# A chunk-attention, top-1 MoE and swish-MLP kernel: the gate in five batches, its matmuls one step later, and the second MLP's first scales and sums beside the last expert tiles

## The chip, the core and the metric

The kernel runs on one core of one Trainium2 chip. The core has a TensorE for matrix products (PE in the rows; PEld is its weight load), a VectorE (DVE), a ScalarE (ACT), a GpSimd (POOL) and a SyncE (SP). Each takes its own instructions in order, and they wait for one another by semaphores. DMA queues move data; here SP and POOL issue them. The metric is the device time of one execution in microseconds; lower is better.

## The reference, cut to what matters

```python
# q, k, v: (8, 8, 576, 64), chunks of 64 positions
scores = 0.125 * q_chunk @ k_chunk.T                 # softmax over 64 keys
x = softmax(scores) @ v_chunk                        # -> tokens: (4608, 512)

xn = x / (norm(x) + 1e-6); en = emb / (norm(emb) + 1e-6)
logits = xn @ en.T / tau                             # (4608, 8)
e = argmax(logits); gate = max of softmax(logits)    # top-1
y = gate * (relu(x @ w1[e]) @ w2[e])                 # 512 -> 1024 -> 512

h = y @ w_in                                         # 512 -> 2048
out = (h / (1 + exp(-1.702 * h))) @ w_out            # 2048 -> 512
```

## The kernel before, in words

Everything is one program without outer loops over data on the chip: its instructions are written out, and each engine executes its own list in the order in which the code emits them.

**The attention front.** A loop over n handles 36 blocks of 128 tokens, as a software pipeline: step n transposes q or k (`emit_T`, matmul L307), makes the scores of block n (L334), transposes the probabilities of n-1 (L357), multiplies those of n-2 with v (L379), and finishes the token tile of n-3 (`end_X`: `x` is scaled into `xr` on POOL at L417 and L418). `emit_XT` (L431) transposes that tile for the gate, `evac_XT` (L439) copies it to `xTa`, and `end_L` issues its gate logits, eight small products with the normalised expert embeddings (L454), into the bank `gb`. Before, `end_L` stands at the end of the same step.

**The gate.** The tiles are gated in batches (`batches`: first tile, count). For a batch, `norm` (16 small DVE operations) and `gate` (some 18 small DVE operations, rank matmuls at L545, an exponential) are generators; `drip` emits about ten pieces of them a step between the operations of attention. The gate's last result is the place of each token in a list sorted by expert. `place` (L494) writes it for one tile by an indirect DMA of POOL into one of two tables `mtab`, even tiles to one, odd tiles to the other, and a write waits until the previous one to its table has landed. `scat` emits one such write. After the loop come the last batch's pieces, with the parts of the first expert tiles' `mm1` and `mm2` in between, and then the last writes (`while scats: scat()`), before `find(3)`.

**The expert stage.** 39 tiles of 128 sorted tokens. `find(i)` (POOL, L851) reads the tables, `fetch(i)` (POOL, L864) gathers the tokens, `turn(i)` (SP) transposes them, `mm1(i)` (PE, L888, 96 products) is relu'd into `hT` by ACT (L895) and DVE (L896), `mm2` (PE, L921, 24 products) is scaled by ACT (L947) and DVE (L948) and scattered back by POOL (L955). `mm2(i-1)` stands behind `mm1(i)`. `swap` splits the next expert's weights into high and low halves where the expert changes (ACT L786, DVE L791; the weights are staged in `stg` and `stgB`).

**The decode.** Beside it, `big_split`, a generator of 32 blocks, turns the second MLP's float64 weights into float16 halves, one block an iteration from i=3 on (`next(dec)`, at the end of the iteration). Block b issues a magnitude for block b+1 on ACT (L1124), `after(b-1)` and four DVE operations. `after` casts on ACT (L1118) and subtracts on POOL (L1127), and the casts wait for the subtractions:

```python
if i == 0:   put(B11, f[0])                          # i is b % 4; put is a cast, then a subtraction
elif i == 1: minus(f[0], f[1], f[0]); put(T1, f[0])
elif i == 2: put(B22, f[2]); minus(f[1], f[2], f[1]); put(T3, f[1])
             minus(f[0], f[2], f[0]); put(T2, f[0])
else:        put(B21, f[3]); minus(f[0], f[3], f[0]); put(T4, f[0])
```

From block 16 on, `after` is one `put`. At iteration LASTD = 36 (NSURE is 3, SURE is 39) the decode ends, its memory is given back, and `prep(0)` loads the first group of the second MLP.

**The second MLP.** Nine groups of 512 tokens. `scales(j)` puts the tokens' scales on a diagonal (DVE L1284), spreads them over the partitions by one matmul (L1286) and copies that (ACT). `sums(j)` makes sums of quarters of the group's tokens (DVE L1297, L1312 to L1324) and splits each into halves `S` (ACT L1301, POOL L1302). `up(j, s)` multiplies them by the weights (PE L1338) and `down` goes back (PE L1451 to L1453). For group 0 both stand before the loop, behind the last expert tile and a `tc.If` (L1236) that catches lists of more than 39 tiles; for the others they stand beside `down` of the group before.

## Time and profile before

| what | value |
|---|---|
| time, median of 3 runs | 1449.27 us (1449.14 to 1451.39) |
| profiled execution, its time | 1442.4 us |
| its span (first to last instruction) | 1440.7 us |
| PE busy in the span | 1300.4 us (90%) |
| DVE, ACT, POOL busy | 855.3, 640.1, 722.7 us |
| mean granted TensorE clock | 0.958 of full speed |

The profile is one execution of the kernel. Its span leaves out 1.7 us of its own time. An engine that is busy 90% of the span bounds it on the whole; what a part of the program waits for is read from its own stretch of the timeline. In timelines, a number in brackets is the time that the engine stood idle before an instruction, and the arrow names what released it.

### The profile page before, as it was taken

How to read it: one execution, taken by the hardware profiler on the slowest of the kernel's cores; microseconds unless marked ns; L12 is line 12 of the kernel's file. 1: busy time of each engine (PE TensorE's matmuls, PEld its weight loads, DVE VectorE, ACT ScalarE, POOL GpSimd, SP SyncE). 2: the span in 40 equal slices, each digit the busy share in tenths (PEclk: the TensorE clock that was granted, in tenths of full speed). 3: DMA queues.
4: the chain of work that ended last, by engine and by line, in shares of the span. 5: the costliest groups of instructions: out<-in, count | busy, mean ns of one | idle time of the engine just before them, and what ended most of it. 6: DMA issues, size and time to landing. Idle time of an engine off the chain costs nothing.

```text
span 1440.7 us, 31953 instructions
## 1 busy us (share of the span) xinstructions
PE 1300.4 (90%) x12802; PEld 915.1 (64%) x12802; DVE 855.3 (59%) x1681; ACT 640.1 (44%) x1125; POOL 722.7 (50%) x648
## 2 busy tenths in 40 slices
...
GB/s 209 216 191 173 167 131 143 68 211 132 209 209 128 162 167 183 255 215 146 69 38 16 45 1 59 2 37 23 23 38 15 45 16 45 9 51 1 30 1 30
DMA packets 196279, 140.71 MB, mean 98 GB/s; under 512 B 129928, under 2 KB 167816, under 8 KB 196112
## 3 DMA queue, kind: packets, MB, share of 16 engines
...
## 4 chain that ended last, share of the span: by engine, by line
PE 50%; DMA 3%; issue 0%; DVE 0%; POOL 0%; ACT 0%; POOLq 0%; DVEq 0%; ACTq 0%
PE pb L1338 6%; PE pd L1338 6%; PE pa L1338 6%; DMA xg<-xs,mt 3%; PE pc L1338 3%; PE gb L1338 3%; PE pa L1453 2%; PE pa L1452 2%; PE pa L1451 2%; PE pd L1451 2%; PE pd L1452 2%; PE pd L1453 2%; PE pb L1452 2%; PE pb L1451 2%; PE pb L1453 2%; PE gb L1452 1%
## 5 line engine op out<-in xcount | busy, mean ns | idle before, releaser
L1338 PEld LDWEIGHTS <-wS 128*128 128x128 f16 x3024 | 297.1, 98 | 42.4 <-issue 5.2
L888 PE MATMUL ph<-xTm,w1HL 128*128 128x128 f16 x3744 | 234.7, 226 | 38.8 <-DMA xTm<-xg 8.1
L888 PEld LDWEIGHTS <-w1HL 128*128 128x128 f16 x3744 | 225.5, 101 | 55.8 <-issue 19.5
L1363 POOL TENSOR_TENSOR w2HL<-z,w1HL 128x512 f16<-128x512 f32 x144 | 217.2, 1524 | 82.8 <-ACT w1HL L1362 81.3
L921 PE MATMUL py<-w2HL,hT 128*128 128x512 f16 x936 | 208.2, 379 | 0.0
L921 PEld LDWEIGHTS <-hT 128*128 128x128 f16 x936 | 89.9, 98 | 101.5
L1458 POOL DMA_INDIRECT out_dram<-y,idc x36 | 35.4, 982 | 235.0 <-ACT y L1457 195.2
L1356 ACT ACTIVATE z<-z 128x512 f32<-128x512 f32 x144 | 88.3, 629 | 107.0 <-DVE z L1353 54.4
L955 POOL DMA_INDIRECT ys<-y,idx_y x39 | 39.1, 1002 | 146.7 <-ACT hT L895 60.1
L1359 DVE TENSOR_TENSOR z<-stgB,z 128x512 f32<-128x512 f32 x108 | 105.3, 1001 | 0.0
L851 POOL DMA_INDIRECT mt<-mtab,idx_g x78 | 88.3, 1132 | 32.9 <-issue 19.7
L1453 PEld LDWEIGHTS <-w2HL 128*128 128x128 f16 x576 | 56.4, 98 | 67.9
L1451 PEld LDWEIGHTS <-w1HL 128*128 128x128 f16 x576 | 56.4, 98 | 67.0
L1452 PEld LDWEIGHTS <-w1HL 128*128 128x128 f16 x576 | 56.4, 98 | 67.0
L1362 ACT ACTIVATE w1HL<-z 128x512 f16<-128x512 f32 x144 | 86.9, 625 | 8.4 <-DVE z L1359 8.4
L417 POOL TENSOR_TENSOR x<-x,sx_all 128x512 f32<-128x512 f32 x33 | 34.3, 1039 | 85.9 <-DVE rd L387 36.8
L896 DVE SCALAR_TENSOR_TENSOR hT<-ph,hT 128x512 f16<-128x512 f32 x78 | 51.0, 683 | 42.8 <-ACT hT L895 40.5
L1175 DVE SCALAR_TENSOR_TENSOR d_f<-raw_o,d_t 128x512 int32<-128x512 int32 x32 | 68.2, 2132 | 3.1
L895 ACT ACTIVATE hT<-ph 128x512 f16<-128x512 f32 x78 | 44.3, 590 | 53.9 <-PE ph L888 49.8
L1384 DVE TENSOR_TENSOR stgB<-stgB,pb 128x512 f32<-128x512 f32 x28 | 19.1, 684 | 81.3 <-PE pb L1338 76.1
L934 ACT ACTIVATE ysq<-py 128x512 f16<-128x512 f32 x39 | 23.1, 593 | 93.8 <-PE py L921 76.2
L1384 DVE TENSOR_TENSOR stgB<-stgB,pd 128x512 f32<-128x512 f32 x27 | 18.5, 684 | 76.4 <-PE pd L1338 76.4
...
## 6 DMA issues: line engine op xcount, KB each, us to landing
...
```

The source lines that it names most:

```text
L851: nc.gpsimd.indirect_dma_start(out=mt_t[i][a][:, :], out_offset=None, in_=mtab[a][:, :], in_offset=bass.IndirectOffsetOnAxis(ap=idx_g[:, i ...
L888: nc.tensor.matmul(p[:, f % 4], wt[:, c, fs], xT[:, a, :], start=(c == 0 and a == 0 and wt is w1H), stop=(c == KD - 1 and wt is w1L),)
L921: nc.tensor.matmul(p, hT[:, a, :], wt[:, c, :], start=st, stop=sp)
L1175: nc.vector.scalar_tensor_tensor(out=fi, in0=hi, scalar=-(1 << 31), in1=t, op0=ALU.bitwise_and, op1=ALU.bitwise_or)
L1338: nc.tensor.matmul(dst, wS[a][:, o, kc, fs], rhs(b, kc), start=first and ab == 0 and kc == 0 and n == 0, stop=(kc == 1 and n == 2), skip_g ...
L1356: nc.scalar.activation(out=z, in_=z, func=AF.Sigmoid, scale=1.702 * 2.0 ** -G_EXP)
L1359: nc.vector.tensor_tensor(out=z, in0=c, in1=z, op=ALU.mult)
L1362: nc.scalar.activation(out=dst[0], in_=z, func=AF.Copy)
L1363: nc.gpsimd.tensor_tensor(out=dst[1], in0=z, in1=dst[0], op=ALU.subtract)
L1451: nc.tensor.matmul(p, gT[0][:, h, c, tt], wo[0][:, c, :], start=(c == 0), stop=False)
L1452: nc.tensor.matmul(p, gT[0][:, h, c, tt], wo[1][:, c, :], start=False, stop=False)
L1453: nc.tensor.matmul(p, gT[1][:, h, c, tt], wo[0][:, c, :], start=False, stop=(c == KG - 1))
```

## The change

Five things are edited in the first two stages and at the seam to the third.

- The gate's batches become five, of 10, 10, 4, 6 and 6 tiles, where they were seven, of 8, 8 and five of 4. The small tiles and the regions of the bank `gb` grow to match. `norm` has one operation fewer: `itau` is multiplied in by `gate`.
- `end_L` of a tile moves from the end of its step to the start of the next one, behind `emit_T` (for n up to 34).
- `scat` is called up to twice at its second place of a step, and the queue of waiting writes is emptied from n = 28 on, where it was 30.
- LASTD becomes 33: `next(dec)` is called twice at i = 6, 8 and 10, so the decode ends, and `prep(0)` starts, three tiles earlier.
- `scales` is cut into `diagonal` and `spread`, and `sums` yields its results to `parts`. For group 0, `diagonal(0)` stands at the end of i = 36, `spread(0)` before `mm2` of tile 36, `early_sums()` at the end of i = 37, and `parts(0)` before `mm2` of tile 37; nothing of them is left behind the `tc.If`. The sums of group 0 lie in memory of their own.

```diff
@@ -439,7 +439,7 @@
...
-    batches = [(0, 8), (8, 8), (16, 4), (20, 4), (24, 4), (28, 4), (32, 4)]
+    batches = [(0, 10), (10, 10), (20, 4), (24, 6), (30, 6)]
@@ -447,7 +447,7 @@
         bi = [j for j, (a, n) in enumerate(batches) if a <= t < a + n][0]
...
-            o = 0 if bi + 1 < len(batches) else 208
+            o = 0 if bi + 1 < len(batches) else 416
             lg_t[bi] = gb[:, o:o + 2 * n * NE].rearrange("p (a e) -> p a e", a=n)
@@ -471,17 +471,15 @@
         yield from rsqrt(y, small("t", n, I32), small("a", n), ssc)
         nc.vector.tensor_tensor(out=y, in0=y, in1=ssc, op=ALU.mult)
         yield
-        nc.vector.tensor_scalar(y, y, 1e-6, None, op0=ALU.add)
+        nc.vector.scalar_tensor_tensor(
+            out=y, in0=y, scalar=1e-6, in1=sx_all[:, t0:t0 + n], op0=ALU.add, op1=ALU.mult
+        )
         yield
...
         isx = is_all[:, t0:t0 + n]
         nc.vector.tensor_scalar(
             isx.bitcast(I32), si_all[:, t0:t0 + n], float((BIAS - X_TOP) << 23), None, op0=ALU.add
-        )
-        yield
-        nc.vector.scalar_tensor_tensor(
-            out=y, in0=y, scalar=itau[:, 0:1], in1=isx, op0=ALU.mult, op1=ALU.mult
         )
         yield
@@ -511,8 +509,9 @@
         l = small("l", n, w=NE)
         nc.vector.tensor_tensor(out=l, in0=lg[:, 0:n, 0:NE], in1=dl, op=ALU.add)
         yield
-        nc.vector.tensor_tensor(
-            out=l, in0=l, in1=rn_all[:, T].unsqueeze(2).to_broadcast([128, n, NE]), op=ALU.mult
+        nc.vector.scalar_tensor_tensor(
+            out=l, in0=l, scalar=itau[:, 0:1], in1=rn_all[:, T].unsqueeze(2).to_broadcast([128, n, NE]),
+            op0=ALU.mult, op1=ALU.mult,
         )
         yield
@@ -539,7 +538,7 @@
         ex = small("ex", n, w=NE)
...
         yield "pe"
-        rkf = gb[:, 128:128 + n * NE]
+        rkf = gb[:, 272:272 + n * NE]
         rk = rkf.rearrange("p (a e) -> p a e", a=n)
         ohf = oh.rearrange("p a e -> p (a e)")
         nc.tensor.matmul(rkf, tri16, ohf, start=True, stop=False)
@@ -990,6 +989,7 @@
     front[LATE + 3] = LATE - 1
     back = {LATE + 2: LATE - 2}
     back.update((t + 3, t) for t in range(LATE, NTILE))
+    turned = []
     for n in range(NTILE + 3):
         now[0] = n
         u, step = n // QR + 1, n % QR
@@ -1003,6 +1003,9 @@
         on(n - 3, emit_sq)
         for f in ev[1]:
             f()
+        if n <= NTILE - 2:
+            for t in turned:
+                end_L(t)
         turned = []
         if n - 1 in back:
             evac_XT(back[n - 1])
@@ -1021,16 +1024,18 @@
         on(n - 1, emit_PT, evac_PT)
         on(n - 2, emit_PV)
         issue_v(v_due(n))
-        if len(scats) > (4 if n < 30 else 0):
-            scat()
+        for _ in range(2):
+            if len(scats) > (4 if n < 28 else 0):
+                scat()
         on(n, exp_S)
         drip(1)
         on(n - 2, emit_x)
         drip(1)
         if n in back:
             emit_XT(back[n])
-        for t in sorted(turned):
-            end_L(t)
+        if n >= NTILE - 2:
+            for t in sorted(turned):
+                end_L(t)
@@ -1192,8 +1197,70 @@
     for b in range(NRAW):
         big_load(b)
     dec = big_split()
+    S_t = [t.bitcast(F16).rearrange("p (l s k t) -> p l s k t", l=2, s=4, k=2) for t in stg_i]
+    def diagonal(j):
+        idc = id_t[j]
+        iv = idc.bitcast(F32)
+        so = mlp.tile([128, 4], F32, tag="so", name="so", bufs=2)
+        nc.vector.tensor_scalar(so, iv[:, :, 1], 2.0 ** (-2 * G_EXP), None, op0=ALU.mult)
+        dg = mlp.tile([128, 4, 128], BF16, tag="dg", name="dg")
+        for a in range(4):
+            nc.vector.tensor_scalar(dg[:, a], identB, iv[:, a, 1:2], None, op0=ALU.mult)
+        id_t[j] = (idc, so)
+        R_t[j] = dg
+    def spread(j, p):
+        nc.tensor.matmul(p, onesB, R_t[j].rearrange("p a t -> p (a t)"), start=True, stop=True)
+        R = mlp.tile([128, 2, 256], BF16, tag="R", name="R", bufs=2)
+        nc.scalar.activation(out=R.rearrange("p a t -> p (a t)"), in_=p, func=AF.Copy)
+        R_t[j] = R
+    def parts(j, i, x):
+        S = S_t[j % 2]
+        nc.scalar.activation(out=S[:, 0, i], in_=x, func=AF.Copy)
+        nc.gpsimd.tensor_tensor(out=S[:, 1, i], in0=x, in1=S[:, 0, i], op=ALU.subtract)
+    def sums(j, quarters, new):
+        yT = yT_t[j]
+        def quarter(r):
+            t = quarters(r).rearrange("p (k t) -> p k t", k=2)
+            nc.vector.tensor_tensor(out=t, in0=yT[:, 2 * r:2 * r + 2], in1=yT[:, KD + 2 * r:KD + 2 * r + 2], op=ALU.add)
+            return t[:, :, 0:256], t[:, :, 256:512]
+        def put(i, x, y, op):
+            o = new(i).rearrange("p (k t) -> p k t", k=2)
+            nc.vector.tensor_tensor(out=o, in0=x, in1=y, op=op)
+            return o
+        a11, a21 = quarter(0)
+        yield
+        a12, a22 = quarter(1)
+        yield
+        s1 = put(0, a21, a22, ALU.add)
+        yield 0, s1
+        s2 = put(1, s1, a11, ALU.subtract)
+        yield 1, s2
+        yield 2, put(2, a11, a21, ALU.subtract)
+        yield 3, put(3, a12, s2, ALU.subtract)
+    def early_sums():
+        w = mlp.tile([128, 2 * KD, 512], F16, tag="yT", name="yT", bufs=2)
+        wf = w.rearrange("p a t -> p (a t)").bitcast(F32).rearrange("p (q t) -> p q t", q=2)
+        z = [
+            mlp.tile([128, 2, 256], F32, tag="z", name="z", bufs=4).rearrange("p a t -> p (a t)")
+            for _ in range(4)
+        ]
+        return [x for x in sums(0, lambda r: wf[:, r], lambda i: z[i]) if x]
     yT_t, id_t, R_t = {}, {}, {}
-    LASTD = NSURE + 33
+    LASTD = NSURE + 30
     for i in range(NSURE, SURE):
         mm1(i)
         if i + 2 < SURE:
@@ -1204,11 +1271,17 @@
             find(i + 4)
         if i + 1 < SURE:
             swap(i + 1, 1)
+        if i == SURE - 1:
+            for n, x in s_0:
+                parts(0, n, x)
+        if i == SURE - 2:
+            spread(0, gb)
         mm2_part(i - 1, 0, KF)
         swap(i, 2)
         mm2_evac(i - 1)
         if i < LASTD:
-            next(dec, None)
+            for _ in range(2 if i in (6, 8, 10) else 1):
+                next(dec, None)
         if i == LASTD:
             next(dec, None)
             dec_stack.close()
@@ -1231,6 +1304,10 @@
                 yT_t[j], id_t[j] = yT, idc
             prep(0)
+        if i == SURE - 3:
+            diagonal(0)
+        if i == SURE - 2:
+            s_0 = early_sums()
     mm2(SURE - 1)
     last = reg(more_i[0:1, 0:1], [ENG.SP, ENG.Activation, ENG.DVE, ENG.PE, ENG.Pool], 1)
@@ -1272,58 +1348,6 @@
...
-    def scales(j):
...
-        p = bank()
-        nc.tensor.matmul(p, onesB, dg.rearrange("p a t -> p (a t)"), start=True, stop=True)
-        R = mlp.tile([128, 2, 256], BF16, tag="R", name="R", bufs=2)
-        nc.scalar.activation(out=R.rearrange("p a t -> p (a t)"), in_=p, func=AF.Copy)
-        R_t[j], id_t[j] = R, (idc, so)
...
-    def sums(j):
-        yT, S = yT_t[j], S_t[j % 2]
...
@@ -1460,22 +1484,28 @@
             in_=o[:, :], in_offset=None,
         )
-    scales(0)
-    for _ in sums(0):
-        pass
+    def spare_q(r):
+        return mem("hT", F32, 1024)
+    def spare_s(i):
+        return mem(("xg", "xTm")[i // 2], F32, 512)
     for j in range(NG):
         for s in range(4):
             up(j, s)
             if s == 0 and j + 1 < NG:
                 prep(j + 1)
         flush()
-        more = sums(j + 1) if j + 1 < NG else iter(())
+        more = sums(j + 1, spare_q, spare_s) if j + 1 < NG else iter(())
         for n, (t, part) in enumerate((t, part) for th in range(2) for part in range(4) for t in (2 * th, 2 * th + 1)):
             down(j, t, part)
             if n > 1:
-                next(more, None)
+                x = next(more, None)
+                if x:
+                    parts(j + 1, *x)
             if n == 10 and j + 1 < NG:
-                scales(j + 1)
+                diagonal(j + 1)
+                spread(j + 1, bank())
```

Three places show how the instructions stand. First PE's list at a step of the front: `db` is the product with v, `tp` a transposition of k, `gb` the gate's logits from the token tile `xTa`, `xr` the next token tile. Before:

```order
L357 MATMUL ptp<-identF,P 128x128 x4
L379 MATMUL db<-vt_91,PT 64x65 x16
L454 LDWEIGHTS xTa
L454 MATMUL gb<-enT,xTa 128x16
...
L454 LDWEIGHTS xTa
L454 MATMUL gb<-enT,xTa 128x16
L307 MATMUL tp<-identF,ku 128x128 x8
L431 LDWEIGHTS xr
L431 MATMUL sp_169<-ident_88,xr 128x128
```

and now:

```order
L357 MATMUL ptp<-identF,P 128x128 x4
L379 MATMUL db<-vt_91,PT 64x65 x16
L307 MATMUL tp<-identF,ku 128x128 x8
L454 LDWEIGHTS xTa
L454 MATMUL gb<-enT,xTa 128x16
...
L454 LDWEIGHTS xTa
L454 MATMUL gb<-enT,xTa 128x16
L431 LDWEIGHTS xr
L431 MATMUL sp_169<-ident_88,xr 128x128
```

The eight pairs of the gate's logits have moved behind the transpositions of the next step.

Second POOL's list at the end of the gate: `mtab` is a table that a placement writes, L851 (now L850) is `find(3)`, and L864 (now L863) the gather of `fetch(3)`. Before:

```order
L789 TENSOR_TENSOR w2HL<-stg_82,w2HL 128x512
L494 DMA mtab_76<-meta,pi_all 36864x2
L494 DMA mtab_77<-meta,pi_all 36864x2
L494 DMA mtab_76<-meta,pi_all 36864x2
L494 DMA mtab_77<-meta,pi_all 36864x2
L851 DMA mt_4372<-mtab_76,idx_g 128x2
L851 DMA mt_4373<-mtab_77,idx_g 128x2
L955 DMA ys<-y,idx_y 4736x1032
L858 TENSOR_TENSOR mt_4372<-mt_4372,mt_4373 128x2
L864 DMA xg<-xs,mt_4372 128x1024
```

and now:

```order
L788 TENSOR_TENSOR w2HL<-stg_82,w2HL 128x512
L492 DMA mtab_76<-meta,pi_all 36864x2
L492 DMA mtab_77<-meta,pi_all 36864x2
L492 DMA mtab_76<-meta,pi_all 36864x2
L492 DMA mtab_77<-meta,pi_all 36864x2
L492 DMA mtab_76<-meta,pi_all 36864x2
L492 DMA mtab_77<-meta,pi_all 36864x2
L850 DMA mt_4271<-mtab_76,idx_g 128x2
L850 DMA mt_4272<-mtab_77,idx_g 128x2
L954 DMA ys<-y,idx_y 4736x1032
L857 TENSOR_TENSOR mt_4271<-mt_4271,mt_4272 128x2
L863 DMA xg<-xs,mt_4271 128x1024
```

Between the last weight operation and `find(3)` stand six placements where there were four; the rows behind them are the same.

Third ACT's list at the end of iteration 8 of the expert loop: `y` is the result of tile 7, `d_t` a magnitude and `wS` a cast of the decode, and `hT` the relu of tile 9, which `mm2(9)` reads and whose evacuation frees the bank for `mm1(10)`. Before:

```order
L830 UNCONDITIONAL_BRANCH
L934 ACTIVATE ysq,ysc<-py_5956 128x512
L947 ACTIVATE y<-py_5956,ysc 128x512
L1124 ACTIVATE d_t<-raw_o_4584 128x512
L1118 ACTIVATE wS_4575<-d_f 128x512
L895 ACTIVATE hT<-ph 128x512 x2
L762 TENSOR_LOAD fl_i
```

and now:

```order
L829 UNCONDITIONAL_BRANCH
L933 ACTIVATE ysq,ysc<-py_5865 128x512
L946 ACTIVATE y<-py_5865,ysc 128x512
L1129 ACTIVATE d_t<-raw_o_4484 128x512
L1123 ACTIVATE wS_4474<-d_f 128x512
L1129 ACTIVATE d_t<-raw_o_4485 128x512
L1123 ACTIVATE wS_4474<-d_f 128x512 x3
L894 ACTIVATE hT<-ph 128x512 x2
L761 TENSOR_LOAD fl_i
```

Between the result of tile 7 and the relu of tile 9 stand two magnitudes and four casts, where one of each stood.

## Rows read from the trace of the kernel before

**Rows 1.** Head of the profile page: span, engines.

```profile
span 1440.7 us, 31953 instructions
...
PE 1300.4 (90%) x12802; PEld 915.1 (64%) x12802; DVE 855.3 (59%) x1681; ACT 640.1 (44%) x1125; POOL 722.7 (50%) x648
```

**Rows 2.** Windows by stage: us, busy (count) of each engine, TensorE clock, DMA.

```profile
39.00:215.00 176.00, 125.34 (x2793) 106.52 (x2793) 147.29 (x445) 129.17 (x246) 92.69 (x88) 0.87 0.81 175
215.00:254.00 39.00, 20.06 (x296) 17.50 (x296) 26.57 (x79) 14.90 (x26) 30.04 (x30) 0.69 0.56 142
...
284.00:529.00 245.00, 214.52 (x2275) 155.95 (x2273) 151.74 (x280) 94.45 (x164) 145.20 (x146) 0.94 0.65 180
...
734.00:1440.00 706.00, 700.48 (x4721) 461.64 (x4718) 349.54 (x448) 271.70 (x471) 337.09 (x248) 1.00 0.10 25
```

**Rows 3.** Windows of two steps of the front.

```profile
57.00:61.50 4.50, 3.57 (x93) 3.09 (x94) 3.65 (x9) 4.23 (x9) 2.21 (x3) 1.00 0.81 205
...
66.90:72.40 5.50, 3.73 (x81) 3.30 (x72) 5.43 (x20) 4.37 (x9) 2.19 (x2) 0.83 0.61 156
```

**Rows 4.** Waits of PE, 39 to 215 us: total, times, longest.

```profile
PE gb L454 <- DVE xTa L439: 11.7, 10, 1.8
PE gb L454 <- DVE si_all L405: 10.9, 11, 1.9
```

**Rows 5.** Timeline of PE, one step: start, duration, [idle before <-releaser].

```profile
54.62 0.36 PE L454 MATMUL gb<-enT,xTa 128*128 128x16 f16 x8 [0.93 <-DVE si_all L405]
54.83 1.07 PE L307 MATMUL tp<-identF,qu 128*128 128x128 f32 x8
```

**Rows 6.** Timeline of POOL, end of the gate.

```profile
262.80 1.34 POOL L494 DMA_INDIRECT mtab<-meta,pi_all  x1 [0.82 <-DVE ttmp L647]
...
266.89 1.31 POOL L494 DMA_INDIRECT mtab<-meta,pi_all  x1 [1.49 <-DMA mtab<-meta,pi_all]
...
272.30 0.99 POOL L851 DMA_INDIRECT mt<-mtab,idx_g  x1 [2.83 <-DVE hT L896]
...
276.98 1.01 POOL L864 DMA_INDIRECT xg<-xs,mt  x1 [0.63 <-issue]
```

**Rows 7.** Timeline of PE, expert tiles 3, 6, 8 and 10.

```profile
283.67 8.02 PE L888 MATMUL ph<-xTm,w1HL 128*128 128x128 f16 x96 [6.60 <-DVE y L951]
...
328.94 5.52 PE L888 MATMUL ph<-xTm,w1HL 128*128 128x128 f16 x96
...
352.72 0.28 PE L888 MATMUL ph<-xTm,w1HL 128*128 128x128 f16 x2 [2.54 <-ACT w1HL L786]
...
378.42 0.27 PE L888 MATMUL ph<-xTm,w1HL 128*128 128x128 f16 x2 [1.12 <-DVE hT L896]
```

**Rows 8.** Timeline of ACT, iterations 6 and 8 of the expert loop.

```profile
342.37 0.61 ACT L1118 ACTIVATE wS<-d_f 128x512 f16<-128x512 f32 x1
...
350.66 1.06 ACT L895 ACTIVATE hT<-ph 128x512 f16<-128x512 f32 x2
...
374.32 1.07 ACT L895 ACTIVATE hT<-ph 128x512 f16<-128x512 f32 x2
```

**Rows 9.** Timeline of PE, expert tiles 19 to 22.

```profile
487.60 0.61 PE L888 MATMUL ph<-xTm,w1HL 128*128 128x128 f16 x8
...
502.43 0.27 PE L888 MATMUL ph<-xTm,w1HL 128*128 128x128 f16 x2 [3.78 <-DVE hT L896]
...
530.01 5.19 PE L888 MATMUL ph<-xTm,w1HL 128*128 128x128 f16 x90
```

**Rows 10.** Timeline of PE, transition to the second MLP.

```profile
721.58 0.39 PE L1286 MATMUL pa<-ysq,onesB 128*128 128x512 bf16 x1 [4.33 <-DVE ysq L1284]
722.19 2.50 PE L1338 MATMUL pc<-yT,wS 128*128 128x256 f16 x12 [0.22 <-issue]
...
733.44 1.47 PE L1338 MATMUL pb<-yT,wS 128*128 128x256 f16 x12
```

**Rows 11.** Timeline of DVE, the same stretch.

```profile
726.20 0.69 DVE L1312 TENSOR_TENSOR xg<-hT 128x512 f32<-128x512 f32 x1 [2.41 <-DMA mt<-mtab,idx_g]
```

41 lines of the change are left out of this document (2 added, 39 removed).

## The prediction, as it was put on record before the changed kernel was run

> **What bounds the kernel now.** I read the head of the page first: PE is busy 1300.4 of 1440.7 us [rows 1], so on the whole the products bound the kernel, and only what lies in the other 140 us, or makes PE slower, can be won or lost. The windows by stage say where these lie [rows 2]. In the second MLP, from 734 us on, PE is busy 700.48 of 706 us: nothing of this change can shorten that. In the front (39 to 215 us) PE is busy 125.34 of 176 us, and DVE, with 147.29 us, is the engine most in use; in the gate's end (215 to 254) it is POOL, with 30.04 of 39. In the first half of the expert stage (284 to 529) PE stands still for 30 of 245 us. So each edit is priced in its own stretch.
>
> **The front.** Here 30 steps take 176 us, 5.87 us each. A step without pieces of the gate takes 4.50 us with 9 operations on DVE (3.65 us busy) and ACT busy for 4.23; a step full of them takes 5.50 with 20 operations, DVE busy 5.43 [rows 3]. Eleven small operations thus cost 1.0 us, 0.09 each. All 445 DVE operations are 30 x 9 = 270 of attention and 175 of the gate: 30 x 4.50 + 175 x 0.09 = 151 us. The remaining 25 us are stalls. PE's table of waits names most of them: the gate's products stand at the end of a step and wait for the token tile just copied, 11.7 us in 10 waits and 10.9 in 11 [rows 4], and behind them in PE's list stand the next step's transpositions, as in the row of 0.93 us of idle time [rows 5].
>
> What the change does to it: fewer batches. By 215 us, five and a half norms and five gates had run; now four norms and three gates, one operation shorter each: I count 126 operations of the gate for 175, that is 49 x 0.09 = 4.4 us less on DVE. With its products behind the transpositions, PE has 1.07 us of other work [rows 5] while the tile is copied, so a plain step falls to what ACT needs, 4.23 us: 0.27 us in some 17 plain steps, 4.6 us. Of the 25 us of stalls I let half go, 12 us, since the waits for the copies go and those for the gate's results come three times in place of five. Together 21 us. Against it: ten placements come at once where there were eight, and POOL now may issue three in one step, each pair of which takes 4.09 us (262.80 to 266.89, [rows 6]), because a write waits for the one before it to its table; POOL also scales the token tiles, and a late `xr` holds PE. That may give back 5 or 6 us. I take **-15**, between -5 (only the operations) and -23 (all these waits of the gate's products gone, 22.6 us). From 215 to 254 us POOL bounds, and its work is the same: 0, give or take 3.
>
> **The gate's end.** The last batch has six tiles, not four, and all six placements stand on POOL ahead of `find(3)` with nothing between them. One pair more is 4.09 us [rows 6]. Behind `find(3)` at 272.30 hang the addition, the gather at 276.98 and the transposition that tile 3 waits for; PE is already idle for 6.60 us there [rows 7], so nothing hides it: **+4.1**. The lower bound is +2.6, if the writes need not wait for the table's former one (two issues at 1.3 us).
>
> **The expert stage.** A tile's period with no wait is 10.54 us (the products of 5.52 us and those of `mm2`, [rows 7]). ACT executes in order, so whatever cast of the decode stands before the relu makes the relu wait, the relu holds the bank of `mm1`, and the next tile's products start late. What one long block costs is shown at iteration 6: the first cast runs at 342.37, the relu only at 350.66 [rows 8], 8.3 us for two subtractions on POOL with their casts, so about 4.1 for each, and PE was idle for 2.54 us before tile 8 [rows 7].
>
> Doubled decode at i = 6 puts block 3's subtraction and cast behind it: 4.1 us and a cast, +4.5. At i = 8 the relu of tile 9 stood behind a single cast of 0.6 us, at 374.32 [rows 8]; now it stands behind four, with three subtractions, which is 8.3 + 3 us in place of 0.6: 10.8 us later. PE's start of tile 10 came at 378.42 behind DVE's half of that relu [rows 7], 3.0 us after ACT's had ended at 375.39, so 3.0 are absorbed: +7.8. At i = 10 only one subtraction is added, but the long blocks fall on i = 11 and 12, where the expert changes and ACT also splits weights: +3.5, from what PE's wait at tile 8, which is such a place too, shows (2.54). These prices hold only as far as the casts are what ends last; if other work hides the chains, they are near 0, which is the other bound.
>
> What is won back: tiles 19 to 21 take 42.41 us from 487.60 to 530.01, where three periods are 31.62, with 3.78 us of idle time behind the relu of tile 19 [rows 9]. There the long blocks 14 and 15 of the decode meet a change of experts. Now these blocks come three iterations earlier, and only single casts stand there: I take -9 of the 10.8.
>
> Last, PE's clock. After 6.60 us of idle time the 96 products of tile 3 took 8.02 us, where they take 5.52 at tile 6 [rows 7]; the two waits that grow to some 7 and 9 us should each cost part of this 2.5: +4. The sum of the stage is 4.5 + 7.8 + 3.5 - 9 + 4, about **+10**, with bounds of +1 (chains half hidden, clock kept) and +18 (nothing absorbed, every wait at the low clock).
>
> [...]
>
> **The seam to the second MLP.** Before, PE waits for 4.33 us at 721.58, spreads the scales in 0.39 us, and between its first products waits for the sums: the fourth product begins at 733.44 [rows 10], 11.86 us after the spread. DVE's first short sum waited for 2.41 us in between, at 726.20 [rows 11]. With sums, scales and halves done beforehand, the three products follow one another: three times 2.50 us, as the first of them took [rows 10], is 7.5 us, or 4.4 at the 1.47 of a later one. I leave the 4.33 us, since the last tile and the `tc.If` still stand ahead. 11.86 - 7.5 is 4.4, 11.86 - 4.4 is 7.5; I take 6. The work that has moved is one product of 0.39 us on PE in tile 37, and on DVE four sums of 0.69 us [rows 11] and two of twice the size (1.4 us each by the elements, an estimate), some 5.6 us behind the evacuation of tile 36. DVE has 38% of its time free in the stage [rows 2], more after the decode's end, so I count 0.5 for PE and the sums together: **-5.5**, between -4 and -7. If the sums were not covered, the relu of tile 38 would hold PE by up to 2 us.
>
> **Sum.** -15 + 0 + 4.1 + 10 - 5.5 = -6.4 us. The profiled execution would take 1442.4 - 6.4 = 1436.0 us; it lies 6.9 us under the median of the runs, so the median comes to 1449.27 - 6.4 = 1443 us. 0.2%, 2.9 us, is about what a measurement of this kernel can tell from no change.
>
> **Rivals.**
> 1. *The doubled decode is hidden.* POOL subtracts the second block's parts while DVE still works, ACT's chain is no longer than before, and the stage gives -5 (the -9, and the +4.5 of tile 8): -15 + 4.1 - 5 - 5.5 is -21, 1428 us. For it: ACT is busy for only 94.45 of 245 us [rows 2]. Against: in 350.66 - 342.37 the time was waiting, not work.
> 2. *The front gives half.* The stalls named for L454 turn into waits of the next instruction in PE's list, because DVE remains the bound: -8, so the sum is +0.6, 1450 us, no change. For it: DVE is busy for 84% of the stretch, and 5.43 of 5.50 us in a full step.
> 3. *Slower: ACT's casts at i = 6, 8 and 10 stand in front of the relu in full.* Nothing is absorbed and each of the lengthened waits starts the next products at the low clock: 4.5 + 10.8 + 3.7 + 3.5 + 5 x 2.5 - 9 = +26 in the expert stage, the sum +10, 1459 us. It decides from +19 in that stage on (15 + 5.5 - 4.1 = 16.4, and 2.9 above). Against it: PE's 3.0 us of slack at tile 10.
>
> **Numbers.** The forecast has 0.42 and a range of its own of 1439 to 1446 us; rival 1 has 0.22, rival 2 has 0.17, rival 3 has 0.19. The forecast and rival 1 are faster by over 0.2%: 0.64; rival 2 is the same: 0.17; slower 0.19. The range of 1426 to 1457 leaves out the lower half of rival 1 and the upper half of rival 3, two in ten.
>
> **What the profile will show.** In the front, L454's waits for `xTa` and `si_all` fall from 22.6 us to under 8, and the stretch that ended at 215 ends near 200. Six placements stand before `find(3)`, 12 us from the first issue to the last's end. The relu of tile 9 runs some 11 us after the first cast at i = 8, with PE idle for 7 to 9 us before tile 10; tiles 19 to 21 have periods under 11.5 us. Behind the `tc.If` PE has no wait for `S`, and three products of 12 follow each other. The prediction is wrong if the front's waits move to the next instruction with their length, or if PE's start of tile 10 does not move against tile 9's.

## The result, and the profile after

The changed kernel takes 1455.49 us (median of 22 runs, 1452.60 to 1460.79) where the kernel before takes 1449.20 (22 runs, 1437.70 to 1461.61). The ratio is 1.006, with a 95% interval of 1.0045 to 1.0075. The two medians lie 6.3 us apart, and 0.6% is 8.7 us: it became slower by 6 to 9 us. Forecast was 1443 us, 6 us faster. The profiled execution has a span of 1454.8 us, 14.1 more than that of before; 5 to 8 us of this belong to the two executions, not to the change.

The head of the page, to compare with [rows 1]:

```profile
span 1454.8 us, 31869 instructions
...
PE 1303.4 (90%) x12800; PEld 914.4 (63%) x12800; DVE 844.4 (58%) x1610; ACT 639.6 (44%) x1123; POOL 722.4 (50%) x648
```

PE is about as busy as before (1303.4 and 1300.4 us), so most of the time went into waits. Three marks part the program: the start of tile 6's products (`mm1`), that of tile 22, and the end. Before they stand at 328.94, 530.01 [rows 7, 9] and 1440.7 us. The timeline of PE after, at tiles 3, 6, 8, 10 and 22:

```profile
292.06 7.42 PE L887 MATMUL ph<-xTm,w1HL 128*128 128x128 f16 x96 [13.81 <-DMA xTm<-xg]
...
336.52 5.52 PE L887 MATMUL ph<-xTm,w1HL 128*128 128x128 f16 x96
...
365.12 0.40 PE L887 MATMUL ph<-xTm,w1HL 128*128 128x128 f16 x2 [7.35 <-ACT w1HL L785]
...
397.48 0.37 PE L887 MATMUL ph<-xTm,w1HL 128*128 128x128 f16 x2 [7.50 <-ACTq L839]
...
549.50 2.67 PE L887 MATMUL ph<-xTm,w1HL 128*128 128x128 f16 x45
```

Up to tile 6 the changed kernel lost 336.52 - 328.94 = 7.6 us. From tile 6 to 22 it took 212.98 us, before 201.07: 11.9 lost. From tile 22 to the end it took 905.3 us, before 910.7: 5.4 won.

**The front.** The window of the same 30 steps, 5 to 34 (they end at 223.5 us, where they ended at 215), and PE's waits in it, in the columns of [rows 2, 4]. They take 186.1 us where they took 176.0:

```profile
37.40:223.50 186.10, 129.22 (x2800) 105.98 (x2804) 135.81 (x396) 126.99 (x244) 97.34 (x94) 0.86 0.76 169
```

```profile
PE sp L431 <- POOL xr L418: 24.4, 7, 6.3
...
PE db L379 <- DMA vt<-in_v_dram: 5.3, 4, 3.0
...
PE gb L454 <- DVE si_all L405: 0.6, 2, 0.4
```

DVE has 49 operations fewer, as counted, and is busy for 11.5 us less. The gate's products wait for almost nothing (`si_all` 0.6 us, and `xTa` is no longer in the list), where 22.6 us stood. But `xr` is now waited for by 24.4 us, in seven waits. Before, the same line of the table was:

```profile
PE sp L431 <- POOL xr L418: 2.5, 2, 2.1
```

What makes `xr` late is seen in POOL's timeline at step 19:

```profile
97.86 1.01 POOL L492 DMA_INDIRECT mtab<-meta,pi_all  x1 [0.16 <-issue]
99.17 1.13 POOL L492 DMA_INDIRECT mtab<-meta,pi_all  x1 [0.30 <-issue]
107.75 0.96 POOL L492 DMA_INDIRECT mtab<-meta,pi_all  x1 [7.45 <-DMA mtab<-meta,pi_all]
108.73 1.06 POOL L417 TENSOR_TENSOR x<-x,sx_all 128x512 f32<-128x512 f32 x1
109.86 1.15 POOL L418 TENSOR_TENSOR xr<-x,xr 128x512 f16<-128x512 f32 x1
```

Two placements are issued in a row at 97.86 and 99.17; the third goes to the table of the first and waits until that one has landed, 7.45 us, and behind it on POOL stand the two scalings of the token tile (L417, L418). PE's product L431 needs `xr` and waits:

```profile
111.07 0.61 PE L431 MATMUL sp<-ident,xr 128*128 128x128 f16 x4 [5.33 <-POOL xr L418]
```

The gate's end, on POOL as in [rows 6]:

```profile
267.22 1.01 POOL L492 DMA_INDIRECT mtab<-meta,pi_all  x1 [0.15 <-DVE qa L674]
...
270.96 0.97 POOL L492 DMA_INDIRECT mtab<-meta,pi_all  x1 [1.30 <-DMA mtab<-meta,pi_all]
...
275.34 0.97 POOL L492 DMA_INDIRECT mtab<-meta,pi_all  x1 [0.30 <-issue]
...
279.61 0.98 POOL L850 DMA_INDIRECT mt<-mtab,idx_g  x1 [0.46 <-DVE ob L691]
```

Six placements take 12.4 us from the first issue to `find(3)`, 2.9 more than the 9.5 of before. But the first of them is issued 43.7 us after the end of step 34 (267.22 - 223.5), before 47.7 (262.80 - 215.1): the gate's work ahead of it began sooner. Two batches are left for the tail in both kernels, but the last but one now ends at tile 29, where it ended at 31: the exponentials of the two stand 3.4 and 32.3 us after the end of step 34 (226.9 and 255.8 us), before 23.8 and 41.0 (238.9 and 256.1). Tile 3 starts 68.6 us after the end of step 34 in both profiles.

**The expert stage.** ACT at the doubled iteration 8, as in [rows 8]:

```profile
382.92 0.69 ACT L946 ACTIVATE y<-py,ysc 128x512 f16<-128x512 f32 x1 [1.75 <-DVE ysc L943]
...
387.59 0.63 ACT L1123 ACTIVATE wS<-d_f 128x512 f16<-128x512 f32 x1 [3.43 <-POOL d_f L1132]
...
395.59 0.63 ACT L1123 ACTIVATE wS<-d_f 128x512 f16<-128x512 f32 x1 [2.48 <-POOL d_f L1132]
396.12 1.07 ACT L894 ACTIVATE hT<-ph 128x512 f16<-128x512 f32 x2
```

Before, the result of tile 7 stood directly ahead of the relu at 374.32 [rows 8]:

```profile
372.66 0.69 ACT L947 ACTIVATE y<-py,ysc 128x512 f16<-128x512 f32 x1 [2.05 <-DVE ysc L944]
```

Between the result of tile 7 (382.92) and the relu of tile 9 (396.12) now lie 13.2 us, where 1.7 lay, and PE stands still for 7.50 us before tile 10. Tiles 19 to 21, which took 42.41 us [rows 9], take 32.56.

**The seam.** PE's timeline behind the last tiles, as in [rows 10]:

```profile
715.85 0.38 PE L1216 MATMUL gb<-dg,onesB 128*128 128x512 bf16 x1
...
732.82 0.38 PE L920 MATMUL py<-w2HL,hT 128*128 128x512 f16 x1 [0.86 <-ACTq L839]
...
742.01 1.74 PE L1362 MATMUL pa<-yT,wS 128*128 128x256 f16 x12 [3.52 <-DVEq L1313]
743.54 2.77 PE L1362 MATMUL pc<-stg,wS 128*128 128x256 f16 x12
746.10 1.67 PE L1362 MATMUL pa<-stg,wS 128*128 128x256 f16 x12
747.60 1.47 PE L1362 MATMUL pb<-yT,wS 128*128 128x256 f16 x12
```

The spread (L1216) has become one product in tile 36, 0.38 us; the first three products of 12 behind the `tc.If` follow one another, and the fourth begins 26.4 us after `mm1` of tile 38 (721.25), before 32.1 (701.36 to 733.44).

### The profile page after: what moved, and what is told of

It is laid out like the page before. It is cut to its first block, busy times and chain, and to the rows that moved or that the text cites. A ratio compares the mean times of both kernels' runs of the same rounds, so it can differ in the third digit from the quotient of the medians.

```text
span 1454.8 us, 31869 instructions
## 1 busy us (share of the span) xinstructions
PE 1303.4 (90%) x12800; PEld 914.4 (63%) x12800; DVE 844.4 (58%) x1610; ACT 639.6 (44%) x1123; POOL 722.4 (50%) x648
## 5 line engine op out<-in xcount | busy, mean ns | idle before, releaser
L850 POOL DMA_INDIRECT mt<-mtab,idx_g x78 | 85.3, 1093 | 28.4 <-issue 20.4
L417 POOL TENSOR_TENSOR x<-x,sx_all 128x512 f32<-128x512 f32 x33 | 34.9, 1057 | 76.0 <-DVE rd L387 38.2
L1180 DVE SCALAR_TENSOR_TENSOR d_f<-raw_o,d_t 128x512 int32<-128x512 int32 x32 | 63.6, 1987 | 3.1
L1377 DVE TENSOR_TENSOR z<-stgB,R 128x512 f32<-128x512 f32 x72 | 58.4, 811 | 7.9 <-POOL z L1377 0.5
L1408 DVE TENSOR_TENSOR stgB<-stgB,pa 128x512 f32<-128x512 f32 x27 | 18.5, 684 | 76.4 <-PE pa L1362 76.4
```

The lines of the kernel that those rows point to most:

```text
L850: nc.gpsimd.indirect_dma_start(out=mt_t[i][a][:, :], out_offset=None, in_=mtab[a][:, :], in_offset=bass.IndirectOffsetOnAxis(ap=idx_g[:, i ...
L1180: nc.vector.scalar_tensor_tensor(out=fi, in0=hi, scalar=-(1 << 31), in1=t, op0=ALU.bitwise_and, op1=ALU.bitwise_or)
```

## The experiments

Every ratio is to the kernel before, run beside it on the same chip, with its 95% interval. The times themselves can't be compared between sets of runs: on one chip the kernel before took 1434.81 us beside runs 1 to 4 and 1447.22 beside runs 5 to 8. The three other columns are from the one profiled execution of each run: the start of tile 6, the time from there to tile 22, and from tile 22 to the end. The same front code put tile 6 at 323.1, 328.9 and 330.6 us in three executions, and that of run 8 at 316.0 to 325.0 in seven, so differences under some 9 us in the first column tell nothing, and the ratio decides. The second column moves as well: six runs with the old decode (before, 4, 6, 9, 12, 14) have 197.3 to 204.2 us, 201.9 in the mean, and seven with the change's doubled decode (changed, 1, 2, 5, 7, 8, 11) have 207.1 to 213.7, 211.3 in the mean. "On 8" means that the kernel of run 8 was edited.

| run | ratio | tile 6 | 6 to 22 | 22 to end |
|---|---|---|---|---|
| before | 1 | 328.9 | 201.1 | 910.7 |
| changed | 1.0060 (1.0045 to 1.0075) | 336.5 | 213.0 | 905.3 |
| 1 one placement at the second place | 1.0094 (1.0065 to 1.0124) | 332.1 | 208.5 | 904.7 |
| 2 back half only | 1.0018 (1.0004 to 1.0032) | 323.1 | 207.1 | 903.5 |
| 3 decode doubled later | 1.0105 (1.0083 to 1.0126) | 341.6 | 197.3 | 909.6 |
| 4 front half only | 1.0073 (1.0057 to 1.0088) | 333.7 | 197.3 | 911.1 |
| 5 changed again | 1.0074 (1.0048 to 1.0100) | 338.1 | 212.2 | 904.3 |
| 6 gate products only | 0.9942 (0.9919 to 0.9964) | 324.2 | 200.6 | 911.0 |
| 7 old gate products | 1.0118 (1.0087 to 1.0149) | 343.4 | 211.5 | 903.0 |
| 8 eight-tile batches | 0.9961 (0.9943 to 0.9979) | 316.0 | 212.8 | 904.1 |
| 9 plain decode on 8 | 0.9954 (0.9931 to 0.9978) | 322.5 | 204.2 | 915.9 |
| 10 casts behind the relu, on 8 | 0.9959 (0.9942 to 0.9975) | 323.8 | 214.9 | 906.5 |
| 11 two placements, on 8 | 1.0013 (0.9991 to 1.0035) | 333.1 | 213.7 | 907.0 |
| 12 seam only | 1.0029 (1.0009 to 1.0050) | 330.6 | 204.2 | 913.8 |
| 13 casts behind the branch, on 8 | 0.9960 (0.9935 to 0.9985) | 320.0 | 214.3 | 905.6 |
| 14 late spread, on 9 | 0.9924 (0.9899 to 0.9949) | 320.7 | 203.8 | 912.3 |
| 15 doubled at 21, 23, 30, on 8 | 0.9970 (0.9948 to 0.9993) | 325.0 | 200.8 | 912.4 |
| 16 doubled at 20, 21, 22, on 8 | 0.9894 (0.9855 to 0.9933) | 322.5 | 202.4 | 906.2 |

A second table sorts the traces by their front code. It has the time of 30 steps, from PE's transposition of the probabilities (L357) in step 5 to that in step 35, and PE's waits for `xr` within it:

| front | runs | 30 steps | waits for `xr` |
|---|---|---|---|
| old | before, 2, 12 | 170.8 to 177.1 | 2.1 to 2.6 |
| gate products moved | 6 | 168.9 | 4.0 |
| moved, eight-tile batches, one placement | 8, 9, 10, 13 to 16 | 166.4 to 172.4 | 5.7 to 8.1 |
| the same with two placements | 11 | 181.9 | 19.0 |
| changed, but one placement | 1 | 182.9 | 19.8 |
| changed | changed, 3, 4, 5 | 184.5 to 191.5 | 24.4 to 33.6 |
| changed, but old gate products | 7 | 193.9 | 22.4 |

Against the third row, the steps of run 11, run 1 and the changed front are longer by about 13, 14 and 19 us, and the waits for `xr` by about 12, 13 and 22.

**1. One placement at the second place of a step, up to n = 27**

```diff
-        for _ in range(2):
+        for _ in range(2 if n >= 28 else 1):
```

> The changed kernel with one thing undone: the second place of a step issues one placement, not two, up to n = 27 (two from n = 28 on). Theory A (the placements on POOL are what the front loses: a third one in a step waits for the landing of the one before it on its table, and the token tile's scaling L417 and L418 stands behind it): the waits of L431 for xr at steps 19 to 21 (8.7 us) fall to under 3 us, the front ends some 6 to 9 us earlier, and the time falls from 1455 to about 1448. Theory B (the front's excess is DVE's work on ten tiles at once, or the moved gate products): POOL's waits go but the step time stays, 1453 to 1456 us.

PE's waits from step 5 to 34, and the two longest for `xr`:

```profile
PE sp L431 <- POOL xr L418: 19.8, 4, 9.3
PE db L379 <- DMA vt<-in_v_dram: 13.1, 6, 4.2
```

```profile
190.70 0.61 PE L431 MATMUL sp<-ident,xr 128*128 128x128 f16 x4 [5.65 <-POOL xr L418]
...
219.67 0.61 PE L431 MATMUL sp<-ident,xr 128*128 128x128 f16 x4 [9.25 <-POOL xr L418]
```

At steps 19 to 21 the waits for `xr` fell from 8.7 to 2.8 us, as theory A says, but the time did not fall: the median of 1448.20 us, which theory A names, stands beside 1434.81 of the kernel before, and the ratio is no better than the changed kernel's. Theory B is not borne out either, since POOL's waits did not go. With the same ten-tile batches the placements are only put off: they pile up at steps 31 and 34 (5.65 and 9.25 us), and waits for v (13.1 us) have taken the place of others. So with ten-tile batches the number a step, before n = 28, is not by itself what costs.

**2. The back half only**: the kernel before with LASTD 33, the doubled decode and the early scales and sums as in the change's diff.

```diff
-    LASTD = NSURE + 33
+    LASTD = NSURE + 30
...
-            next(dec, None)
+            for _ in range(2 if i in (6, 8, 10) else 1):
+                next(dec, None)
...
+        if i == SURE - 3:
+            diagonal(0)
+        if i == SURE - 2:
+            s_0 = early_sums()
```

> Only the back half of the change: the kernel before with LASTD 33, the decode doubled at 6, 8 and 10, and the early scales and sums; batches, gate products and placements as before. By the two traces, tiles 5 to 22 lose 12 us and the seam wins 6: +6 us, about 1455 us. Rival (the front alone makes the change slower, the stage's loss is an accident of one execution): the seam's 6 us show, 1443 us.

Slower by 2.6 us, less than the 6 expected; both terms are there: 7.2 us won from tile 22 on, and tiles 6 to 22 cost 9.8 us more than in run 4, which has the old decode. The size of this loss is uncertain by some us: against run 12, which is this very kernel with the old decode, it is 2.9, and by the two means above 9.4.

**3. The decode doubled at 21, 23 and 30**

```diff
-            for _ in range(2 if i in (6, 8, 10) else 1):
+            for _ in range(2 if i in (21, 23, 30) else 1):
```

> The changed kernel with the decode doubled at iterations 21, 23 and 30 in place of 6, 8 and 10, where every block is a single cast. If the long blocks doubled at 6 and 8 hold the relu: tiles 7 to 10 come back to the periods of before (13.25, 13.49, 12.21, 11.92), 12 us are won, about 1443 us. Rival (long blocks cost the same wherever they meet a change of experts; only their place moves): tiles 19 to 21 lose again the 7 to 9 us that were won there, 1451 to 1454 us.

The early tiles came back as expected (13.25, 13.75, 11.96 and 11.10 us for tiles 7 to 10). Tiles 19 to 21 took 40.3 us where the changed kernel has 32.56, so the rival's loss of 7 to 9 us is there as well, within the sum of 197.3 us. Another 4 us are lost later, at tiles 25 and 32 (12.97 us each), where the weights of the next expert are split. The ratio shows nothing of the difference of some 10 us that remains; no run of the changed kernel stood in the same set, and this stays open. What the columns show is the stage alone.

**4. The front half only**: the changed kernel with the decode, the scales and the sums of before.

```diff
-    LASTD = NSURE + 30
+    LASTD = NSURE + 33
...
-            for _ in range(2 if i in (6, 8, 10) else 1):
-                next(dec, None)
+            next(dec, None)
...
+    scales(0)
+    for _ in sums(0):
+        pass
```

> Only the front half of the change: batches, gate products, placements; decode, scales and sums as before. By the two traces the start of tile 5 came 7.6 us later (318.40 against 325.98): if that is the change and not the execution, about 1456 us. If the front is neutral and the expert stage alone costs: 1449 us. As I predicted it (-15 + 4): 1438 us.

0.73%, 10 us slower, where the forecast's terms for this half say 11 us faster: the front's loss is the change's. 1.0073 and 1.0018 together give 1.009; the whole has 1.006 and 1.0074.

**5. The changed kernel again**, with no edit.

> The changed kernel once more, as it is, on the chip of the next three runs. If its parts add up as the front half alone (ratio 1.0073) and the back half alone (1.0018) say, the ratio is 1.009, 13 us; by the 22 runs it is 1.006, 9 us. Its profile shows whether the front's end (end of step 34 at 223.5 us) and its waits for xr (24.4 us) come again: within 4 us if they belong to the kernel.

The end of step 34 lies at 228.6 us, and PE's waits from step 5 to there are:

```profile
PE sp L431 <- POOL xr L418: 32.3, 8, 7.7
```

The waits come again, but not within the 4 us that were expected: they are 7.9 us longer than in the first profile, and the front ends 5.1 us later. Their size depends on the execution too.

**6. The gate's products only**, in the kernel before

```diff
+        if n <= NTILE - 2:
+            for t in turned:
+                end_L(t)
...
-        for t in sorted(turned):
-            end_L(t)
+        if n >= NTILE - 2:
+            for t in sorted(turned):
+                end_L(t)
```

> The kernel before with one thing done: the gate's products one step later. Theory P (what the front loses are the placements, which the ten-tile batches push together; the moved products win): the waits of L454 for xTa and si_all go (over 20 us), the waits for xr stay near 2.5 us, and the front ends 6 to 12 us earlier, ratio about 0.994. Theory D (the front is paced by its loads; whatever a step saves comes back as waits for v and k): waits for vt and ku grow to what is saved, the time stays, ratio 1.000.

PE's waits from 39 to 215 us:

```profile
PE sp L431 <- POOL xr L418: 4.0, 1, 4.0
PE gb L454 <- DVE g_po L572: 4.0, 3, 1.9
```

Theory P: 0.58%, 8.4 us faster. The waits of L454 for `si_all` and `xTa` fell from 22.6 us to under 2, that for `xr` is 4.0 us in one wait. Of the 22.6 us, a third has reached the end.

**7. The old gate products in the changed kernel**

```diff
-        if n <= NTILE - 2:
-            for t in turned:
-                end_L(t)
...
-        if n >= NTILE - 2:
-            for t in sorted(turned):
-                end_L(t)
+        for t in sorted(turned):
+            end_L(t)
```

> The changed kernel with the gate's products back at the end of their step. Theory P: the placements are pushed together as before, xr is waited for by some 20 us, and the waits of L454 come back: 5 to 10 us slower than the changed kernel, ratio about 1.013. Theory D (the loads pace the front, and running ahead of them is what costs): the steps fall back to the pace of the loads and nothing is lost against the changed kernel, ratio 1.006 to 1.009.

PE's waits in steps 5 to 34:

```profile
PE sp L431 <- POOL xr L418: 22.4, 7, 7.3
```

L454 waits again for `si_all` and `xTa`, 22.7 us in 21 waits. Both waits are there, as theory P says. By the ratios it is 0.44% slower than the changed kernel beside it, 6.4 us (5.2 by the medians): the moved products win in both fronts. Theory D falls.

**8. Batches of eight, one placement**

```diff
-    batches = [(0, 10), (10, 10), (20, 4), (24, 6), (30, 6)]
+    batches = [(0, 8), (8, 8), (16, 4), (20, 4), (24, 6), (30, 6)]
...
-        for _ in range(2):
-            if len(scats) > (4 if n < 28 else 0):
-                scat()
+        if len(scats) > (4 if n < 30 else 0):
+            scat()
```

> The changed kernel with batches of 8, 8, 4, 4, 6 and 6 tiles and one placement at the second place of a step, so that the first 24 tiles are placed as before; gate products one step later, doubled decode and early sums as changed. Theory P: the waits for xr fall from 24 to under 8 us and the front ends some 12 us earlier than in the changed kernel: ratio 0.997 to 0.999. Theory D: the waits move to vt and ku, the front ends within 4 us of the changed kernel's, ratio 1.006.

PE's waits for `xr` in steps 5 to 34:

```profile
PE sp L431 <- POOL xr L418: 7.3, 2, 4.2
```

16 us (1.13%) faster than the changed kernel beside it, a little more than theory P expected. If the parts add up, and the back half (1.0018) is taken off, the front with six batches stands at 0.994, as in run 6 with seven, and the second table has the two at the same time: fewer batches and the shorter norm are worth nothing that shows.

**9. The decode not doubled, on run 8**

```diff
-    LASTD = NSURE + 30
+    LASTD = NSURE + 33
...
-            for _ in range(2 if i in (6, 8, 10) else 1):
-                next(dec, None)
+            next(dec, None)
```

> The kernel of the run with eight-tile batches, with the decode not doubled (LASTD 36, one block an iteration, as before); sums, diagonal and spread early as in the change. If the doubled blocks are what the expert stage loses, the start of tile 22 comes 208 to 212 us after tile 5's (it is 223.3 in that run), and the seam keeps its 6 us: ratio 0.988 to 0.990. If the early sums need the three tiles that the doubled decode wins for them (the first group's loads come too late in tile 36), the seam gives back 3 us or more: ratio 0.991 to 0.993.

Tiles 6 to 22 fell by 8.6 us, but tile 37 takes 18.4 us. The ratio of 0.9954 is above both cases of the expectation: nothing was won. PE there:

```profile
690.91 5.52 PE L887 MATMUL ph<-xTm,w1HL 128*128 128x128 f16 x96
702.40 0.61 PE L1215 MATMUL gb<-dg,onesB 128*128 128x512 bf16 x1 [5.97 <-DVE dg L1209]
702.80 6.70 PE L920 MATMUL py<-w2HL,hT 128*128 128x512 f16 x24
709.34 2.84 PE L887 MATMUL ph<-xTm,w1HL 128*128 128x128 f16 x48
```

The spread waits 5.97 us for the diagonal, whose scales `prep(0)` has only just loaded, and `mm2` and `mm1` stand behind it. So the doubled decode pays for something: the early scales need `prep(0)` three tiles earlier.

**10. The second block's casts behind the relu, on run 8**

```diff
     for i in range(NSURE, SURE):
         mm1(i)
+        if i in (7, 9, 11):
+            next(dec, None)
...
-            for _ in range(2 if i in (6, 8, 10) else 1):
-                next(dec, None)
+            next(dec, None)
```

> The same kernel with the decode doubled, but the second block of each doubled pair issued behind mm1 of the next iteration, so that its casts stand behind the relu on ACT, where they stood ahead of it. Theory of the chain (what costs is that the relu stands behind three more casts that wait for POOL): tiles 7 and 9 fall from 18 us to under 14.5, tiles 5 to 22 take 212 to 216 us, ratio 0.991 to 0.993. Rival (it is the work itself, on DVE and POOL, that the stage has no room for): the wait moves to the weights' split at tiles 8 and 12 or to the results, tiles 5 to 22 stay at 221 to 224 us, ratio 0.996.

Nothing came back (214.9 us; 225.4 from tile 5), and the ratio of 0.9959 is the rival's. PE at tiles 8 and 10, and ACT's relu of tile 9 with what follows:

```profile
352.26 0.39 PE L887 MATMUL ph<-xTm,w1HL 128*128 128x128 f16 x2 [7.18 <-ACT w1HL L785]
...
385.59 4.61 PE L887 MATMUL ph<-xTm,w1HL 128*128 128x128 f16 x52 [8.39 <-ACTq L839]
```

```profile
375.49 1.06 ACT L894 ACTIVATE hT<-ph 128x512 f16<-128x512 f32 x2
...
383.89 0.63 ACT L1122 ACTIVATE wS<-d_f 128x512 f16<-128x512 f32 x1 [2.94 <-POOL d_f L1131]
385.90 0.60 ACT L933 ACTIVATE ysq<-py 128x512 f16<-128x512 f32 x1 [1.39 <-ACTq L839]
```

The relu now runs at 375.49, but tile 10 begins at 385.59, released by ACT's sequencer at the branch of `swap` (L839), which stands behind the last cast. My chain, in which the relu is what PE waits for, falls: behind the relu stands a branch whose passing PE waits for as well, and at tile 8 the split of the weights. Whether the rival is right as well, that the stage has no room for the work of two blocks, this run does not tell.

**11. Two placements at the second place, on run 8**

```diff
-        if len(scats) > (4 if n < 30 else 0):
-            scat()
+        for _ in range(2):
+            if len(scats) > (4 if n < 28 else 0):
+                scat()
```

> The changed kernel with batches of 8, 8, 4, 4, 6 and 6 tiles, two placements at the second place as changed. It parts the size of the batches from the rate: if the ten tiles at a time are the cause, the waits for xr stay near 11 us and the ratio near 0.996; if the second placement of a step is, they go to over 18 us and the ratio to 1.002 or more.

```profile
PE sp L431 <- POOL xr L418: 19.0, 4, 7.5
```

19.0 us of waits for `xr` in four waits, and by the two ratios 0.52% (7.5 us) slower than run 8, which ran on another chip: the second placement, with the earlier emptying of the queue, costs with eight-tile batches too. With run 1, either of the two alone, ten-tile batches or the second placement, brings most of the waits.

**12. The seam only**: run 2 with the decode as before.

```diff
-    LASTD = NSURE + 30
+    LASTD = NSURE + 33
...
-            for _ in range(2 if i in (6, 8, 10) else 1):
-                next(dec, None)
+            next(dec, None)
```

> The kernel before with only the seam changed: diagonal, spread, sums and halves of group 0 early; batches, gate products and decode as before (LASTD 36). By the row of the back half alone (1.0018) and its expert stage's 9.8 us, the seam is worth 6 to 7 us: ratio 0.9955. As predicted, 5.5 us: 0.996. If the late first group holds the early sums, under 3 us: 0.998 or more.

Slower, the third case and beyond it: tile 37 takes 18.3 us as in run 9.

**13. The second block behind the branch, on run 8**

```diff
         if i + 1 < SURE:
             swap(i + 1, 1)
+        if i in (7, 9, 11):
+            next(dec, None)
...
-            for _ in range(2 if i in (6, 8, 10) else 1):
-                next(dec, None)
+            next(dec, None)
```

> As the run with the casts behind the relu, but the second block of each doubled pair now stands behind the branch of the weights' exchange (swap of the next tile) as well. If PE's wait before tiles 8 and 10 is for ACT to pass that branch and its splits, which stood behind the casts in every order so far: tile 9's period falls from 19.1 us to under 13, tile 7's from 17.9 to under 14.5, tiles 5 to 22 take 211 to 216 us in place of 225.5, ratio 0.988 to 0.991. Rival (the stage has no room for the work of two blocks, whatever the order): the wait moves to the evacuation of the results, tiles 5 to 22 stay above 221 us, ratio 0.996.

Tiles 7 and 9 fell to 13.25 and 12.97 us, as the first theory says, and tiles 8, 10 and 12 rose to 16.40, 19.51 and 18.29. PE at tile 10:

```profile
373.19 0.27 PE L887 MATMUL ph<-xTm,w1HL 128*128 128x128 f16 x2 [1.71 <-DVE hT L895]
...
383.47 6.96 PE L920 MATMUL py<-w2HL,hT 128*128 128x512 f16 x24 [3.41 <-ACTq L839]
392.71 0.27 PE L887 MATMUL ph<-xTm,w1HL 128*128 128x128 f16 x2 [2.28 <-ACTq L839]
```

Now `mm2` waits for ACT's next branch and the tile after for the one behind it; 214.3 us as before. In three orders (runs 8, 10 and 13) the sum stayed within 2.1 us. Tiles 5 to 22 took 224.9 us and the ratio is 0.9960, so the rival's numbers came true, though the waits did not move to the evacuation of the results, as it says.

**14. The spread one tile later, on run 9**

```diff
         if i == SURE - 1:
             for n, x in s_0:
                 parts(0, n, x)
-        if i == SURE - 2:
             spread(0, gb)
```

> The run with the plain decode (LASTD 36), with the spread of group 0's scales one tile later, ahead of mm2 of tile 37, where its diagonal has been ready for some 6 us. If the spread on PE was what made tile 37 take 18.4 us there: 10.8 us now, 7.6 us won, ratio 0.989 to 0.991. If the sums' late data holds DVE as well (the relu of tile 38 behind sums that wait for the first group's loads): tile 37 or 38 keeps over 4 of the 7.6 us, ratio 0.993 or more.

Tile 37 takes 12.2 us, but the next `mm2` waits 3.65 us, and nothing of the seam's gain shows (912.3). The ratio lies between the two cases of the expectation. Even so this kernel, with the old decode, is 0.36% faster by the ratios than run 13 beside it (1437.40 and 1441.60 us), which has the doubled decode and the seam's gain.

**15 and 16. The doubled decode at iterations with single casts, on run 8**

```diff
-            for _ in range(2 if i in (6, 8, 10) else 1):
+            for _ in range(2 if i in (20, 21, 22) else 1):
```

This is run 16; run 15 has (21, 23, 30).

> The eight-tile front and the early sums, with the decode doubled at iterations 21, 23 and 30, where every block is a single cast (in the third run, on the changed front, tiles 5 to 22 took 207.9 us so, and tiles 22 to 38 5.4 us more than in the changed kernel). If parts add up: tiles 5 to 22 take 208 to 211 us, tiles 22 to 38 176 us, the seam keeps 6 us: ratio 0.990. If the eight-tile front's better start is what the expert stage then loses (its loads come too late): 0.994 or more.

> The same with the doubled iterations 20, 21 and 22, ahead of the next change of experts at tile 24. If two light blocks cost only where they meet the split of the next expert's weights on DVE (tiles 25 and 32 took 12.97 us so): tiles 22 to 38 fall to 171 to 172 us, ratio 0.987. If two light blocks do not fit one tile's 10.54 us on DVE at all: tiles 20 to 23 take 12 us each, 5 us more, ratio 0.990 as with the other three.

Run 15 loses at tile 25 (14.34 us) and 32 (12.97). Run 16 keeps clear of the changes of experts and has the seam's gain. Its tiles 22 to 38 take 172.8 us, about what the first case says, and the ratio is the second case's. It has the lowest ratio here, though its interval meets that of run 14: 0.9894, 1431.08 us in the median where the kernel before had 1444.95 beside it.

## Why the prediction was wrong

The forecast of 1443 us was 12 us too low, and the change went the other way; the range of 1426 to 1457 us holds the median all the same. By its terms:

- **The front, -15.** This is the step that failed, and with it the sentences "Together 21 us" and "That may give back 5 or 6 us". The front half alone, with the gate's end, costs 10 us (run 4) where -15 and +4.1 were forecast; the back half alone costs 2.6 us (run 2) where +10 and -5.5 were.
  - *What is gained.* It was there in direction: plain steps take 4.20 us where 4.23 was forecast, L454's waits for `xTa` and `si_all` fell from 22.6 us to under 1, DVE has the 49 operations fewer. But the gain that reached the end is 8.4 us (run 6), not 21, and comes from the moved products alone.
  - *What is given back.* The batches and placements together cost some 16 us (run 8 against 5), not 5 or 6. I priced a wait by the pair at the gate's end, 4.09 us, and counted it once. Where a placement waited for the one before it to its table, it started, in the profiles before and after, 4.76 to 10.62 us after that one's issue in the front (ten cases), 5.47 to 12.07 between the front and the last batch (five), and 3.74 to 5.53 in the last batch (four). Each wait holds the scaling of a token tile, so the waits for `xr` rose by 22 us.
  - *What I overlooked.* Ten-tile batches bunch the placements: those of tiles 10 to 19 are issued from 157.6 to 189.5 us. Between two scalings POOL had at most two placements up to 196 us, and now has three, several times in a row, and the six gathers of three `find`s stand together ahead of a scaling at the end of step 34 (210.0 to 217.9 us), where before scalings stood between them.
  - *The rivals.* The sign that was named for being wrong, waits that move to the next instruction with their length, came: 22.6 us at L454 became 24.4 at L431. But they are not the same waits, and not DVE's, as rival 2 has it: in run 6 those of L454 go and those for `xr` hardly come, and in run 7 both are there. Rival 3's 1459 us lies nearest to the measured time by luck, since it puts the loss into the expert stage.
- **The gate's end, +4.1.** The lengthening is 2.9 us on POOL, and nothing reached tile 3: the gate's work ahead of the placements began sooner. I took the start of the first placement as fixed.
- **The expert stage, +10.** It measured 11.9 us in the two profiles, 9.8 between runs 2 and 4, and 9.4 between the means of seven and six runs. The size was right, the nine won back at tiles 19 to 21 (9.9) also; tile 9's period rose by 6.0 us where 7.8 were forecast, and PE stood for 7.50 us before tile 10, where 7 to 9 were. The relu of tile 9 came 8.5 us after the first cast, not 11. The mechanism was only half right: the casts hold ACT, but PE waits for what stands behind them on ACT whatever that is, the relu, the weights' split or the branch (runs 10 and 13). No engine is full there: from 347 to 441 us, where the three doubled blocks fall, PE is busy 77% and DVE, the next, 73% (the row below, in the columns of [rows 2]). That speaks for the chain between the engines, and against a lack of time on one of them. But no run parts the length of the chain from the amount of work: run 16, whose tiles 6 to 22 take 202.4 us, no more than with the old decode, doubles blocks that have less of both.

```profile
347.00:441.00 94.00, 72.09 (x737) 52.83 (x735) 68.17 (x107) 42.95 (x70) 61.91 (x58) 0.88 0.63 172
```

- **The seam, -5.5.** 5.4 in the two profiles, 7.2 between run 2 and the kernel before. The idle time ahead of the first product stayed, as assumed (4.33 us before, 3.52 now). That the early scales hang on the doubled decode (runs 9 and 12) stood nowhere in the forecast.
- **The clock, +4 within the stage.** The term was an estimate from tile 3's row alone. It was about 2.4, with no run that parts it from the rest of the stage. From tile 6 to 22 PE was busy 181.74 us where it was 179.32, with as many products, at a mean granted clock of 0.94 where it was 0.97 (the rows below, before and after). A longer wait did not always cost more: tile 3's products took 7.42 us after 13.81 us of idle time, and 8.02 after 6.60 before.

```profile
328.94:530.01 201.07, 179.32 (x1921) 128.98 (x1920) 138.41 (x248) 85.81 (x148) 126.60 (x125) 0.97 0.61 171
336.52:549.50 212.98, 181.74 (x1921) 131.74 (x1920) 145.64 (x260) 90.67 (x154) 129.86 (x128) 0.94 0.61 168
```

What stays open: why a placement lands so late in the front, whether for the loads beside it or for the table's write itself (it did so in the kernel before too, 4.98 to 8.74 us in four cases, where the placements were not bunched); and why runs 1 and 3, of one set, are slower by the ratio than their columns say.
